# New prices for VectorE's two-operand sums and GpSimd's broadcast products in the table that orders a kernel's queues

## The chip, the cores and the metric

The kernel runs on one core of one Trainium2 chip. The metric is the device time of one execution in microseconds (us). Five queues matter: TensorE (PE in the profile, with its weight loads as PEld), VectorE (DVE), ScalarE (ACT), GpSimd (POOL), and SyncE (SP), which issues the DMA transfers. Each queue runs its instructions in the order in which they stand in it; an instruction whose input isn't ready holds up all behind it.

## What is computed

Eight sequences of 4224 positions with 192 channels. A dynamic convolution with seven taps per position and head (eight heads of 24 channels), the taps normalised by a softmax; then the real part of a two-dimensional Fourier transform added to its own input; then a layer norm and a two-layer perceptron (192 to 768 to 192) with a second residual:

```python
w = np.exp(weight_gen - max)                      # softmax over the 7 taps
w = w / (np.sum(w, axis=-1, keepdims=True) + 1e-09)
x = einsum('bshk,bskhg->bshg', w, x_unfolded)     # dynamic convolution
X = np.fft.fft(x, axis=1)
X = np.fft.fft(X, axis=2)
u = x + np.real(X)
un = (u - mu) / np.sqrt(var + 1e-06)
ch = np.maximum(un @ w_ch1, 0.0) @ w_ch2
return u + ch
```

The inputs are float32; the two weight matrices come as float64 words, which the kernel turns into float32 and then into pairs of float16 (a high and a low part) with a common scale.

## The kernel before

**The stages of a batch.** The 4224 positions of a batch lie as 128 partitions by 33 rows. Batches follow each other as a pipeline: while the perceptron of one batch runs on TensorE, the convolution of the next runs on VectorE and GpSimd.

1. *Taps* (`softmax_taps`, `scale_taps`): VectorE takes maxima, differences, sums and reciprocals of the taps, ScalarE the exponential. For the first two batches this goes by parts (lines 573 to 582), for later ones the maxima and differences (573, 574) are made for the whole batch at once and the sums by quarter (822 to 825). Line 693 scales the taps of the chunks whose products GpSimd makes alone.
2. *Convolution* (`conv` for batches 0 and 1, `wide_conv` from batch 2): a product of the rows with one tap, broadcast over a head's 24 channels, and a sum of the seven. Products are VectorE's (line 762, 768 elements wide; line 847, 1536 wide) or, for a few chunks of batches 0 and 1, GpSimd's (line 760). Sums are GpSimd's (lines 771 and 851); in batch 1, from the third chunk on, the first sum of each chunk is VectorE's (`DVE_ADDS`, also line 771: six of them). In batch 0 TensorE makes some sums.
3. *Fold and spectrum*: GpSimd folds the rows (794, 795), TensorE makes the first transform over positions (pg, line 803), ScalarE and VectorE combine it (809; 810, 813) into gt, which goes to DRAM and comes back in another layout as g (line 889).
4. *Transform*: TensorE's second transform (pp, line 899), copied by ScalarE into pq (903 to 914).
5. *Mix*: TensorE's transform over channels (eo, line 930); ScalarE copies one half (ot, line 935), VectorE adds it to u (936 to 939, 943, 944).
6. *Norm*: ScalarE takes the two statistics of the four rows of a group (lines 965 and 967, one pass per row, into "junk"), a root (969), the normalised rows (996) and their float16 part (1000); GpSimd takes the rest of the parts (1001, 1003); a DMA transposes them into ht.
7. *Perceptron*: nine groups per batch. TensorE makes ph (lines 1060 and 1027), ScalarE evicts it through the ReLU as hh (1075 or 1079; VectorE's line 1080 takes the low part from the eighth group of the program on), TensorE makes po (1094), VectorE adds it to u (1099), and u is stored. PSUM has three banks for ph, two for po, two for transforms and mixes ("fft"), one for the taps of a batch.

The weights of the second layer are turned into float32 (w2f), scaled by their maximum (lines 446 to 461) and split into w2h and w2l (line 489 makes w2l on VectorE, three instructions), while the perceptron of batch 0 runs on w2f.

**What sets the order of the queues.** The program is written stream by stream. At its end `plan` reorders every queue: `cost` gives each instruction two numbers, how long it holds its queue and when its result is there; `walk` then places all instructions one by one by these numbers, the dependencies, the free buffers and banks and a rank. It goes backward and forward over the program ten times, ranks by the lateness that the last pass found, keeps the order with the least total, and ties each queue to that order. So a number in `cost` changes no instruction, only places. For VectorE the number is 150 ns and 1.042 ns for each element of a partition, for GpSimd 183 ns and 2.13 ns (1.92 ns with a float16 output).

Of the kernel before, what the change touches and what calls it, by code (L numbers as in the profile page):

```python
# [11 lines left out]
F16 = mybir.dt.float16  # L12
# [72 lines left out]
def area(ap, kind):  # L85

    if kind == "psum":
        return (0, P), [(0, 1)]
    dims, base, parts, size = [list(d) for d in ap.ap], ap.offset, (0, 1), BYTES[ap.dtype]
    if kind != "dram":  # L90
        step, n = dims.pop(0)
        parts, base = ((base // step, base // step + n), base % step) if step else ((0, P), base)
    free, run = [], 1
    for step, n in dims:
        base += min(step, 0) * (n - 1)
        if n > 1 and step:
            free.append((abs(step), n))
    free.sort(reverse=True)
    while free and (free[-1][0] <= run or np.prod([n for _, n in free]) > 80):
        step, n = free.pop()  # L100
        run += step * (n - 1)
    spans = [base]
    for step, n in free:
        spans = [b + step * k for k in range(n) for b in spans]
    if len(spans) == 2 and run >= 4 * 192:
        spans, run = [min(spans)], run + max(spans) - min(spans)
    return parts, sorted((b * size, (b + run) * size) for b in spans)


def meet(a, b):  # L110

    (pa, sa), (pb, sb) = a, b
    if pa[0] >= pb[1] or pb[0] >= pa[1] or sa[0][0] >= sb[-1][1] or sb[0][0] >= sa[-1][1]:
        return False
    i = j = 0
    while i < len(sa) and j < len(sb):
        if sa[i][0] < sb[j][1] and sb[j][0] < sa[i][1]:
            return True
        if sa[i][1] <= sb[j][1]:
            i += 1  # L120
        else:
            j += 1
    return False


def covers(a, b):

    (pa, sa), (pb, sb) = a, b
    return len(sa) == 1 and pa[0] <= pb[0] and pb[1] <= pa[1] and sa[0][0] <= sb[0][0] and sb[-1][1] <= sa[0][1]


def together(ap):

    run = 1
    for step, n in reversed(ap.ap[1:]):
        if n > 1 and step != run:
            break
        run *= n
    return run


def cost(ins, lane, reads, writes):

    count = lambda ap: int(np.prod([n for _, n in ap.ap[1:]]))
    out = writes[0]
    n = max(map(count, reads + writes))
    if lane == "pe":
        n = count(out)
        t = 2 * max(112 if 64 < n <= DH else 56, 0.855 * n) if reads[0].dtype == F32 else max(55.8, 0.417 * n + 2.4)
        if reads[0].dtype == F16 and reads[0].ap[0][1] == P // 2:  # L150
            t = HALF
        return t, t + 178
    if lane == "sp":
        if ins.opcode == "DmaTransposeAnt":
            return TURN, 2000 + 1.2 * n, 1.09 * n
        size, run = BYTES[out.dtype], min(together(ap) for ap in reads + writes)
        return 400, 2000 + WIRE * count(out) * size, out.ap[0][1] * count(out) / run * (0.5 + 0.0023 * run * size)
    if lane == "dve":
        t = 150 + (6.27 if ins.opcode == "Reciprocal" else 1.042) * n + (60 if len(reads) == 3 and n < 512 else 0)
        return t - 83, t  # L160
    if lane == "pool":
        t = 183 + (1.92 if out.dtype == F16 else 2.13) * n
        return t - 45, t
    t = 190 + (0.833 if out.ap[-1][0] == 1 else 1.666) * n + 90 * (len(reads) - 1)
    return (t + 100, t + 90) if len(writes) > 1 else (t - 95, t)


def plan(nc, tc, homes, holds, glued, opening):

    ops, index = [], {}  # L170
    writers, readers, users = defaultdict(list), defaultdict(list), defaultdict(list)
    rows = defaultdict(list)
    for at, ins in enumerate(nc.cur_bb.bb.instructions):
        reads, writes = ([a.bass_ap for a in args if hasattr(a, "bass_ap")] for args in (ins.ins, ins.outs))
        if ins.engine not in LANES or not writes:
            continue
        joined = ins.name in glued
        k, lane = index.setdefault(ins.name, len(ops) - joined), LANES[ins.engine]
        spots = [(ap.tensor.name, area(ap, homes[ap.tensor.name][0]), w)
                 for w, aps in ((0, reads), (1, writes)) for ap in aps if ap.tensor.name in homes]  # L180
        needs = {}
        for name, spot, w in spots:
            psum = homes[name][0] == "psum"
            for old, sync in ((writers[name], True), (readers[name], w)):
                for other, j in old if sync or psum else ():
                    if j != k and (psum or meet(spot, other)):
                        needs[j] = needs.get(j, False) or sync
        for name, spot, w in spots:
            kind, tag, bufs = homes[name]
            if name not in users and bufs and kind != "dram":  # L190
                rows[kind, tag].append(name)
            users[name].append(k)
            if w and homes[name][0] != "psum":
                for old in (writers, readers):
                    old[name] = [(other, j) for other, j in old[name] if not covers(spot, other)]
            (writers if w else readers)[name].append((spot, k))
        for lo, hi, first in holds:
            if lo <= at < hi and first.engine == ins.engine:
                needs.setdefault(index[first.name], False)
        price = cost(ins, lane, reads, writes)  # L200
        if joined:
            line, _, paid, wants, names = ops[k]
            for j, sync in needs.items():
                wants[j] = wants.get(j, False) or sync
            ops[k] = (line + [ins], lane, (paid[0] + price[0], paid[0] + price[1]), wants, names | {n for n, _, _ in spots})
        else:
            ops.append(([ins], lane, price, needs, {n for n, _, _ in spots}))
# [139 lines left out]
def tile_dynconv_fnet_mlp(  # L347
# [859 lines left out]
    for b in range(B):  # L1207
# [6 lines left out]
        for g in range(NG):  # L1214
            if b > 0 or g >= QUICK:
                at = t0 - mix_at + step * g + (0.7 if b == 0 else 0)
                add(at, at + step, late_mix(g) if b == 0 and g >= QUICK else mix(b, g))
                add(max(at + step, t0 + g - 2.0), t0 + g - 1.0, norm(b, g))
    run()
    plan(nc, tc, homes, holds, glued, last_pq0)  # L1220


# [35 lines left out]
```

## Time and profile before

| | |
|---|---|
| runs | 1088.95, 1089.6, 1089.92 us (median 1089.6) |
| span of the profiled execution | 1087.9 us; 1.7 us of the median lie around it |
| instructions | 23453 |
| TensorE busy | 1065.5 us (98%) |
| VectorE busy | 958.7 us (88%) |
| GpSimd busy | 857.1 us (79%) |
| ScalarE busy | 800.0 us (74%) |
| DMA queue, share of 16 engines | 45.2% |

The profile is that of one execution. Its page has busy times by engine, the span in 40 slices, the chain of waits that ended last, and the costliest groups of instructions. The trace behind it was read by stretches of time, by line, and as a timeline of single instructions. A row of the timeline has the start (us), the length (us), the engine, the line, the operation, and output<-inputs with their shapes; in brackets stands how long the engine stood idle just before, and whose result ended that. Busy times of TensorE are of pipelined matmuls and somewhat generous.

### The profile page before, as it was taken

What the parts mean: (1) busy time and instruction counts of PE and PEld (TensorE: products, weight loads), DVE (VectorE), ACT (ScalarE), POOL (GpSimd) and SP (SyncE); (2) the same over time, 40 slices, a digit from 0 to 9 for tenths busy, and PEclk for the clock granted to TensorE, in tenths of its full rate; (3) what the DMA queues carried; (4) which work ended last, traced back from release to release, by engine and by line L of the source; (5) the groups of instructions that cost most, each with busy time, mean ns of one, the idle gap of its engine ahead of it and who ended that gap; (6) DMA issues with size and microseconds to landing.
All of it is one profiled execution on the core that took longest, in us unless ns stands there. A gap on an engine that the chain in (4) does not pass through costs nothing.

```text
span 1087.9 us, 23453 instructions
## 1 busy us (share of the span) xinstructions
PE 1065.5 (98%) x8600; PEld 802.9 (74%) x8600; DVE 958.7 (88%) x1639; ACT 800.0 (74%) x2414; POOL 857.1 (79%) x615
## 2 busy tenths in 40 slices
PE   7899999999999999999999999999999999999998
PEld 5477777787767877777778876887778777786767
DVE  8999999899989999899999999899999998355543
ACT  4666864679966878788786877678786878588842
POOL 5989699899969999799969999699969999011200
PEclk9999999999999999999999999999999999999999
DMA  9353135714492348623582348624582333623311
GB/s 323 129 146 115 34 94 141 202 46 111 119 259 80 85 115 206 170 67 85 129 248 79 92 109 220 157 57 121 122 205 68 83 68 89 140 56 76 79 53 48
DMA packets 171091, 131.20 MB, mean 121 GB/s; under 512 B 119067, under 2 KB 151776, under 8 KB 170976
## 3 DMA queue, kind: packets, MB, share of 16 engines
q1 hardware_dynamic: 170976, 129.70, 45.2%
q8 instruction: 68, 1.11, 0.4%
q14 instruction: 47, 0.39, 0.1%
HBM read 61.46 MB, written 39.37 MB: 93 GB/s over the span
## 4 chain that ended last, share of the span: by engine, by line
PE 66%; DVE 14%; POOL 5%; DMA 4%; ACT 3%; issue 3%; SPq 0%; DVEq 0%; ACTq 0%; POOLq 0%
PE po L1094 27%; PE ph L1060 24%; PE pp L899 5%; PE eo L930 4%; PE ph L1027 3%; DVE pr L847 3%; POOL u L771 2%; PE pg L803 2%; DVE hh L1080 2%; ACT pr L723 1%; DMA ht<-hl 1%; DVE pr L762 1%; POOL u L851 1%; DMA g<-g_d 1%; DMA ring<-ht 1%
## 5 line engine op out<-in xcount | busy, mean ns | idle before, releaser
L851 POOL TENSOR_TENSOR u<-u,pr 128x1536 f32<-128x1536 f32 x144 | 497.0, 3452 | 5.5 <-DVE pr L847 1.7
L1094 PE MATMUL po<-w2h,hh 128*128 128x192 f16 x2832 | 409.2, 247 | 0.0
L1094 PEld LDWEIGHTS <-hh 128*128 128x128 f16 x4248 | 359.1, 98 | 60.1 <-issue 15.2
L1060 PE MATMUL ph<-ht,w1h 128*128 128x512 f16 (+1 forms) x1296 | 382.7, 362 | 0.3 <-ACT ht L987 0.3
L1094 PE MATMUL po<-w2l,hh 128*128 128x192 f16 x1416 | 348.8, 246 | 0.0
L1080 DVE SCALAR_TENSOR_TENSOR hh<-ph,hh 128x512 f16<-128x512 f32 (+1 forms) x390 | 240.5, 636 | 60.9 <-ACT hh L1079 60.5
L1079 ACT ACTIVATE hh<-ph 128x512 f16<-128x512 f32 (+1 forms) x390 | 206.0, 550 | 89.2 <-PE ph L1060 41.0
L847 DVE TENSOR_TENSOR pr<-x_sb,wp 128x1536 f32<-128x1536 f32 x144 | 249.7, 1747 | 7.3 <-POOL u L851 7.3
L1060 PEld LDWEIGHTS <-w1h 128*128 128x128 f16 x1296 | 125.3, 98 | 97.9 <-issue 9.4
L1060 PE MATMUL ph<-ht,w1l 128*128 128x512 f16 (+1 forms) x528 | 181.7, 350 | 0.0
L996 ACT ACTIVATE un<-u,rs 128x192 f32<-128x192 f32 x252 | 122.2, 539 | 40.2 <-POOL rs L994 34.5
L1001 POOL TENSOR_TENSOR hl<-un,hl 128x512 f16<-128x512 f32 (+1 forms) x69 | 74.9, 1086 | 84.3 <-issue 42.5
L771 POOL TENSOR_TENSOR u<-u,pr 128x768 f32<-128x768 f32 (+1 forms) x72 | 117.9, 1649 | 12.2 <-DVE pr L762 11.4
L967 ACT ACTIVATE junk<-u,st 128x192 f16<-128x192 f32 x252 | 114.3, 453 | 4.4
L965 ACT ACTIVATE junk<-u 128x192 f16<-128x192 f32 x252 | 90.8, 360 | 27.6 <-DVE u L939 21.8
L1099 DVE SCALAR_TENSOR_TENSOR u<-po,isc,u 128x384 f32<-128x384 f32 (+1 forms) x122 | 73.1, 599 | 21.1 <-PE po L1094 20.7
L930 PEld LDWEIGHTS eo<-cs_sb,pq 97*128 97x128 f32 x544 | 78.3, 191 | 13.4 <-issue 4.4
L930 PE MATMUL eo<-cs_sb,pq 97*128 97x97 f32 x544 | 85.7, 275 | 0.0
L762 DVE TENSOR_TENSOR pr<-x_sb,wp 128x768 f32<-128x768 f32 (+1 forms) x91 | 74.7, 868 | 2.1 <-POOL u L771 0.7
L1060 PEld LDWEIGHTS <-w1l 128*128 128x128 f16 x528 | 51.9, 98 | 21.6 <-issue 0.5
L794 POOL TENSOR_TENSOR sm<-u 128x382 f32<-128x382 f32 x64 | 64.6, 1009 | 3.7 <-ACT u L779 3.2
L994 POOL TENSOR_TENSOR rs<-st,rs 128x4 f32<-128x4 f32 (+1 forms) x69 | 13.6, 201 | 67.4 <-DVE rs L970 67.3
(130 smaller groups left out, 1538.4 us busy)
## 6 DMA issues: line engine op xcount, KB each, us to landing
out_dram<-u SPq DMA_DIRECT2D x64, 384.0 KB
x_sb<-in_x_dram SPq DMA_DIRECT2D x48, 384.0 KB
g<-g_d SPq DMA_DIRECT2D x40, 336.0 KB
x_sb<-in_x_dram SPq DMA_DIRECT2D x8, 864.0 KB
g_d<-gt SPq DMA_DIRECT2D x32, 195.0 KB
g_d<-gt SPq DMA_DIRECT2D x32, 189.0 KB
w<-in_weight_gen_dram SPq DMA_DIRECT2D x6, 924.0 KB
x_sb<-in_x_dram SPq DMA_DIRECT2D x8, 672.0 KB
```

The source lines that it names most:

```text
L762: last_product[b] = nc.vector.tensor_tensor(out=dst, in0=rows, in1=wk, op=ALU.mult)
L771: adder.tensor_tensor(out=u, in0=u, in1=pr, op=ALU.add)
L847: last_product[b] = nc.vector.tensor_tensor(out=pr.rearrange("p (s r) (h g) -> p s (r h) g", s=2, g=G), in0=rows, in1=wp[:, :, :, k:k + 1] ...
L851: nc.gpsimd.tensor_tensor(out=u, in0=u, in1=pr, op=ALU.add)
L930: last_mix[b] = nc.tensor.matmul(eo[:, e, j, :], lhsT=pq[0:DH, e, r, r:r + P], rhs=cs_sb[:, e, :], start=True, stop=True)
L965: nc.scalar.activation(junk, uv[t], AF.Identity, scale=-1.0 / D, accum_out=st[:, t, 0:1])
L967: nc.scalar.activation(junk, uv[t], AF.Square, bias=st[:, t, 0:1], accum_out=st[:, t, 1:2])
L996: nc.scalar.activation(un[:, t, :], uv[t], AF.Identity, bias=rs[:, 1, t:t + 1], scale=rs[:, 0, t:t + 1])
L1060: last_ph[n] = nc.tensor.matmul(ph[:, 0:T], lhsT=wt[:, cs_], rhs=ht[:, 0:T, blk], start=(i == 0 and not opens), stop=(i == len(terms) - 1 ...
L1079: nc.scalar.activation(a[:, 0:T], ph[:, 0:T], AF.Relu)
L1080: nc.vector.scalar_tensor_tensor(out=l[:, 0:T], in0=ph[:, 0:T], scalar=0.0, in1=a[:, 0:T], op0=ALU.max, op1=ALU.subtract)
L1094: nc.tensor.matmul(po[t // 2][:, t % 2, :], lhsT=hx[:, t], rhs=wx[:, c2, :], start=(c2 == 0 and i == 0), stop=(c2 == NH - 1 and i == len(t ...
```

## The change

`cost` gets the names of all tiles that don't lie in PSUM. A VectorE instruction that reads exactly two operands of more than 64 elements, both of them outside PSUM and neither broadcast along its last axis, is priced at 2.0 ns per element in place of 1.042. A GpSimd instruction with a broadcast operand is priced at 1.78 ns per element in place of 2.13. All else is as before.

```diff
-def cost(ins, lane, reads, writes):
+def cost(ins, lane, reads, writes, sbuf):
...
     if lane == "dve":
-        t = 150 + (6.27 if ins.opcode == "Reciprocal" else 1.042) * n + (60 if len(reads) == 3 and n < 512 else 0)
+        slow = len(reads) == 2 and n > 64 and all(ap.tensor.name in sbuf and ap.ap[-1][0] for ap in reads)
+        t = 150 + (6.27 if ins.opcode == "Reciprocal" else 2.0 if slow else 1.042) * n + (60 if len(reads) == 3 and n < 512 else 0)
         return t - 83, t
     if lane == "pool":
-        t = 183 + (1.92 if out.dtype == F16 else 2.13) * n
+        t = 183 + (1.92 if out.dtype == F16 else 1.78 if any(ap.ap[-1][0] == 0 for ap in reads) else 2.13) * n
         return t - 45, t
...
-    rows = defaultdict(list)
+    rows, sbuf = defaultdict(list), {name for name, home in homes.items() if home[0] != "psum"}
...
-        price = cost(ins, lane, reads, writes)
+        price = cost(ins, lane, reads, writes, sbuf)
```

The first rule meets the six adds of line 771 in batch 1; the second meets the nineteen products of line 760 in batches 0 and 1, and two small products of tap tables. Line 489 reads three operands (w2f, a scale, w2h) and keeps its price. The two programs hold the same instructions; from the 61st place on TensorE's queue and the 67th on VectorE's the order differs nearly everywhere by a few places, and TensorE's last 915 or so are the same again. The changed kernel's lines are higher by one (the eviction of line 1075 is line 1076). Three places follow. A row has the line, the operation, and output<-inputs with their tiles' names and running numbers.

ScalarE, near the end of the perceptron's second group: hh_1_4 and hh_1_5 are its last two evictions, rs_3 and un_3 the norm of group 3, junk_4 the passes over the rows of group 4, ot_5 a copy of a mix. Before:

```order
L969 ACTIVATE rs_3_1225<-st_3_1224,eps_t 128x4
L996 ACTIVATE un_3_1227<-u_2_228,rs_3_1225 128x192 x4
L1000 CAST hl_3_1273<-un_3_1227 128x4x192
L1075 ACTIVATE hh_1_4_1302<-ph_1_4_1296 128x512
L1075 ACTIVATE hh_1_5_1314<-ph_1_5_1308 128x512
L935 COPY ot_5_1400<-eo_5_1358 128x194
L965 ACTIVATE junk_4_1341,st_4_1339<-u_4_337 128x192 x3
L1075 ACTIVATE hh_2_0_1328<-ph_2_0_1322 128x512
```

And with the change:

```order
L997 ACTIVATE un_3_1227<-u_2_228,rs_3_1225 128x192 x4
L936 COPY ot_5_1400<-eo_5_1358 128x194
L1001 CAST hl_3_1273<-un_3_1227 128x4x192
L966 ACTIVATE junk_4_1341,st_4_1339<-u_4_337 128x192 x4
L968 ACTIVATE junk_4_1341,st_4_1339<-u_4_337,st_4_1339 128x192 x4
L970 ACTIVATE rs_4_1340<-st_4_1339,eps_t 128x4
L1076 ACTIVATE hh_1_4_1302<-ph_1_4_1296 128x512
L1076 ACTIVATE hh_1_5_1314<-ph_1_5_1308 128x512
```

The eight passes of group 4 and their root moved ahead of the two evictions; before they stood between the evictions that follow.

VectorE, where the scale of the second layer's weights is made and the taps of batch 2 begin (w_2042 are these taps; po_3_1 the second half of the output of group 3). Before:

```order
L1099 SCALAR_TENSOR_TENSOR u_2_228<-po_3_1_1730,sc_w_879,u_2_228 128x384
L461 TENSOR_SCALAR sc_w_1803<-m_w_1796 128x1
L459 TENSOR_SCALAR sc_w_1803<-m_w_1796 128x1
L529 TENSOR_TENSOR isc<-sc_w_879,sc_w_1803 128x1
L762 TENSOR_TENSOR pr_8_3_2009<-x_sb,wp_815 128x192 x2
L762 TENSOR_TENSOR pr_8_5_2016<-x_sb,wp_815 128x192 x2
L573 TENSOR_REDUCE wp_2041<-w_2042 128x264
L574 TENSOR_TENSOR w_2042<-w_2042,wp_2041 128x1848
```

And with the change:

```order
L763 TENSOR_TENSOR pr_8_3_2009<-x_sb,wp_815 128x192 x2
L763 TENSOR_TENSOR pr_8_5_2016<-x_sb,wp_815 128x192 x2
L574 TENSOR_REDUCE wp_2041<-w_2042 128x264
L575 TENSOR_TENSOR w_2042<-w_2042,wp_2041 128x1848
L1100 SCALAR_TENSOR_TENSOR u_2_228<-po_3_1_1730,sc_w_879,u_2_228 128x384
```

The add of po_3_1, which gives its bank free, moved behind the last products of batch 1 and the two wide rows of the taps; the scale rows moved further back still.

VectorE, in the first quarter of batch 2's convolution (pr_0_3 to pr_0_6 are products 1536 wide; w2l the low part of the second layer's weights). Before:

```order
L847 TENSOR_TENSOR pr_0_3_2189<-x_sb,wp_2041 128x1536
L1099 SCALAR_TENSOR_TENSOR u_4_337<-po_4_1_1914,sc_w_879,u_4_337 128x384
L847 TENSOR_TENSOR pr_0_4_2235<-x_sb,wp_2041 128x1536
L1099 SCALAR_TENSOR_TENSOR u_4_337<-po_5_0_1975,sc_w_879,u_4_337 128x384
L847 TENSOR_TENSOR pr_0_5_2266<-x_sb,wp_2041 128x1536
```

And with the change:

```order
L848 TENSOR_TENSOR pr_0_3_2189<-x_sb,wp_2041 128x1536
L1100 SCALAR_TENSOR_TENSOR u_4_337<-po_4_1_1914,sc_w_879,u_4_337 128x384
L848 TENSOR_TENSOR pr_0_4_2235<-x_sb,wp_2041 128x1536
L490 SCALAR_TENSOR_TENSOR w2l<-w2f,sc_w_1803,w2h 128x384
L1100 SCALAR_TENSOR_TENSOR u_4_337<-po_5_0_1975,sc_w_879,u_4_337 128x384
L490 SCALAR_TENSOR_TENSOR w2l<-w2f,sc_w_1803,w2h 128x384 x2
L848 TENSOR_TENSOR pr_0_5_2266<-x_sb,wp_2041 128x1536
```

The three w2l rows, which stood as one run nine places ahead of the batch's first product (u_0), moved in between its fifth and sixth.

## Prediction

> **What bounds the kernel now.** I read the head of the page first, then the windows of the span by stage, then the groups of waits.
>
> ```profile
> span 1087.9 us, 23453 instructions
> PE 1065.5 (98%) x8600; PEld 802.9 (74%) x8600; DVE 958.7 (88%) x1639; ACT 800.0 (74%) x2414; POOL 857.1 (79%) x615
> ```
>
> TensorE is busy for 98% of the span and every other engine has air over the whole of it. A new order issues the same matmuls, so it can win only what PE loses in waits, and it loses only where some new wait reaches PE. Where those waits are, the windows say (start and end in us, length, busy time of each engine):
>
> ```profile
> core 0: us, PE busy (x) PEld busy (x) DVE busy (x) ACT busy (x) POOL busy (x), PEclk, DMA share, GB/s
> 0.00:100.00 100.00, 89.12 (x445) 62.35 (x446) 92.95 (x191) 56.86 (x225) 82.91 (x73) 0.98 0.60 194
> 100.00:205.00 105.00, 100.19 (x562) 75.77 (x562) 102.00 (x178) 72.82 (x189) 93.69 (x77) 1.00 0.36 98
> 205.00:935.00 730.00, 727.13 (x6249) 552.32 (x6248) 691.77 (x1130) 572.91 (x1710) 663.76 (x440) 1.00 0.49 125
> ```
>
> PE is idle for 10.9 us in the head (filling, loads), for 105 − 100.19 = 4.8 us in 100 to 205, where the second batch is convolved, and for 730 − 727.13 = 2.9 us in all the steady part. In 100 to 205 VectorE is busy for 102.00 of 105 us: there the two engines bound each other, and there all repriced instructions stand. A better order can thus gain about 4.8 + 2.9 = 7.7 us at the very most outside the head; a worse one has no such bound. The waits of PE by kind (sum, count, longest):
>
> ```profile
> PE po L1094 <- DVE u L1099: 2.2, 2, 1.4
> PE pg L803 <- POOL sm L795: 2.1, 3, 1.3
> PE pp L899 <- DMA g<-g_d: 1.5, 2, 0.9
> PEld pp L899 <- DMA g<-g_d: 1.4, 1, 1.4
> ```
>
> The first two are of the stretch 100 to 205, the last two lie where a batch's transform begins.
>
> **What is repriced.** The rule for VectorE meets six instructions, the adds of line 771 in batch 1: the walk counted 150 + 1.042 × 768 = 950 ns for each, and now 150 + 2.0 × 768 = 1686. The rule for GpSimd meets the products of line 760: 183 + 2.13 × 768 = 1819 ns, now 1550. In the trace (count, shortest/median/longest ns):
>
> ```profile
> L771 DVE TENSOR_TENSOR u<-u,pr x6: 958/1698/2411, 122.0 to 175.6; 128x768 f32<-128x768 f32 x6
> L760 POOL TENSOR_TENSOR pr<-x_sb,w x12: 1542/1580/1593, 72.5 to 108.2; 128x768 f32<-128x768 f32 x12
> L489 DVE SCALAR_TENSOR_TENSOR w2l<-w2f,sc_w,w2h x3: 603/605/953, 194.3 to 195.7; 128x384 f16<-128x384 f32 x3
> L851 POOL TENSOR_TENSOR u<-u,pr x144: 3422/3452/3486, 204.4 to 911.3; 128x1536 f32<-128x1536 f32 x144
> ```
>
> Both new prices are better averages. The product's is a constant of the instruction (1542 to 1593). The add's is not: 958 to 2411 ns for one shape is a wait, and the timeline shows for what:
>
> ```profile
> 142.15 1.83 POOL L771 TENSOR_TENSOR u<-u,pr 128x768 f32<-128x768 f32 x1
> 142.38 2.41 DVE L771 TENSOR_TENSOR u<-u,pr 128x768 f32<-128x768 f32 x1
> 143.92 1.88 POOL L1001 TENSOR_TENSOR hl<-un,hl 128x512 f16<-128x512 f32 x1
> ```
>
> ```profile
> L1001 POOL TENSOR_TENSOR hl<-un,hl 128x512 f16<-128x512 f32 x61 | 71.5, 1172 | 75.8 <-ACT hl L1000 38.3 <-issue 34.1 <-DMA ht<-hl 2.8
> ```
>
> VectorE's add starts at 142.38 inside GpSimd's add, which ends at 143.98; the add ends at 144.79, 0.81 us later, so it did its work after GpSimd's. GpSimd's next instruction takes 1.88 us where its group's mean is 1.172: it stood behind the VectorE add in turn. So an add costs about 0.96 us plus what is left of GpSimd's instruction, and the table now holds the mean of that. The instructions themselves become neither shorter nor longer; only places in the queues change. The rest is what the moves cost.
>
> [...]
>
> **The moves, one by one.**
>
> *VectorE, 70 us: the tap scaling of batch 1.* The two line-693 rows now stand behind about eleven rows of the first weight preparation, some 4.5 us later. GpSimd's first product of batch 1 waits for the first of them, so GpSimd's run of products starts later by that. It is covered: after those products GpSimd has nothing to do until VectorE's products arrive.
>
> ```profile
> 70.50 0.39 DVE L693 TENSOR_TENSOR w<-w,wp 128x224 f32<-128x224 f32 x1
> ...
> 123.94 1.82 POOL L771 TENSOR_TENSOR u<-u,pr 128x768 f32<-128x768 f32 x1 [8.41 <-DVE pr L762]
> ```
>
> The wait of 8.41 us shrinks to about 4. Cost **0**; without that cover 4.5 us.
>
> *ScalarE, 83 us.* The weight conversion of line 488 goes ahead of the copies of the transform's fifth piece, and the chain copies, first mixes, first norm stands behind it.
>
> ```profile
> 83.49 0.58 ACT L488 ACTIVATE w1h<-pw_w,sc_w 128x384 f16<-128x384 f32 x1 [0.50 <-DVE pw_w L483]
> 91.30 0.32 ACT L935 COPY ot<-eo 128x194 f32<-128x194 f32 x1 [0.78 <-PE eo L930]
> 92.02 0.36 DVE L936 TENSOR_TENSOR eo<-eo,ot 128x194 f32<-128x194 f32 x1
> ```
>
> The copies are pushed by 0.58 to 1.08 us (the conversion, with or without its own wait); VectorE takes the first mix 92.02 − 91.62 = 0.40 after it is ready, so 0.2 to 0.7 us comes through. I take **+0.4**.
>
> *ScalarE, 128 to 134 us.* Before, the evictions of ph_1_4 and ph_1_5 start at 128.70 and the eight statistics passes of group 4 are spread between later evictions. Now all eight, and the root behind them, stand ahead of these evictions.
>
> ```profile
> 128.70 1.09 ACT L1075 ACTIVATE hh<-ph 128x512 f32<-128x512 f32 x2
> 130.23 0.36 ACT L965 ACTIVATE junk<-u 128x192 f16<-128x192 f32 x1
> 130.72 0.36 ACT L965 ACTIVATE junk<-u 128x192 f16<-128x192 f32 x1
> 131.45 0.38 PE L1060 MATMUL ph<-ht,w1h 128*128 128x512 f16 x1
> 138.84 0.61 DVE L1099 SCALAR_TENSOR_TENSOR u<-po,sc_w,u 128x384 f32<-128x384 f32 x1
> 139.11 0.46 ACT L967 ACTIVATE junk<-u,st 128x192 f16<-128x192 f32 x1
> 139.59 0.73 PE L1094 MATMUL po<-w2f,hh 128*128 128x192 f32 x3 [1.36 <-DVE u L1099]
> 145.38 0.92 PE L1094 MATMUL po<-w2f,hh 128*128 128x192 f32 x4 [0.80 <-DVE u L1099]
> ```
>
> A first pass takes 0.49 from start to start (130.23, 130.72), a second 0.46 and the same gap of 0.13. Four of each: 1.96 + 2.36 = 4.3 us; with the mix's copy (0.32, row at 91.30) and as much for the root 4.9, so the first eviction ends near 128.70 + 4.9 + 0.55 = 134.2. PE wants that bank at 131.45: a new wait of 2.75 us. In return VectorE's line 1099 moves ahead by several rows, from 138.84 to about 134.6, and both po waits of 1.36 and 0.80 end. Net **+0.6**; bounds +2.75 (they stay) and −2.2 (the eviction is no later).
>
> *But GpSimd sets the pace here.* These +1.0 us stand ahead of a wait that GpSimd decides:
>
> ```profile
> 175.13 0.92 PE L803 MATMUL pg<-sm,f_sb 128*128 128x192 f32 x4 [1.33 <-POOL sm L795]
> ```
>
> Of the 105 us from 100 to 205 GpSimd is idle for 11.3, and 8.4 of these are the gap before 123.94: from there on it hardly stops, and its own order is the same but for a few places. PE arriving 1.0 us later waits 0.33 us instead of 1.33. So of the two terms **0** is left; if GpSimd's sum comes later too, +1.0.
>
> *VectorE, 187 to 194 us: one bank given back late.* Line 1099 of po_3_1 now stands behind the two rows that begin the tap softmax of batch 2.
>
> ```profile
> 187.22 0.60 DVE L1099 SCALAR_TENSOR_TENSOR u<-po,sc_w,u 128x384 f32<-128x384 f32 x1
> 189.49 2.09 DVE L573 TENSOR_REDUCE wp<-w 128x264 f32<-128x1848 f32 x1
> 191.61 2.08 DVE L574 TENSOR_TENSOR w<-w,wp 128x1848 f32<-128x1848 f32 x1
> 192.41 0.33 PE L1094 MATMUL po<-w2f,hh 128*128 128x192 f32 x1
> ```
>
> Those two end at 193.69 now; without line 1099 and the four small scale rows ahead of them (1.1 us) at about 192.6. Line 1099 then ends at 193.2, and PE's po_4_1, which takes this bank, is due at 192.41. Wait: **+0.9** with the hop (bounds 0, if PE is late itself, and +2.2, if the 1.1 us is not won).
>
> *VectorE, 207 to 217 us: the w2l splits.* Three line-489 rows, which ran among short GpSimd rows at 194.3 to 195.7, now stand between the products of batch 2's first quarter, beside GpSimd's adds of 3.45 us.
>
> ```profile
> 207.91 1.75 DVE L847 TENSOR_TENSOR pr<-x_sb,wp 128x1536 f32<-128x1536 f32 x1 [0.90 <-POOL u L851]
> 211.71 1.75 DVE L847 TENSOR_TENSOR pr<-x_sb,wp 128x1536 f32<-128x1536 f32 x1 [1.51 <-POOL u L851]
> 215.37 1.75 DVE L847 TENSOR_TENSOR pr<-x_sb,wp 128x1536 f32<-128x1536 f32 x1 [1.91 <-POOL u L851]
> ```
>
> VectorE waits here for GpSimd, 0.90 + 1.51 + 1.91 = 4.3 us in three gaps, and the splits' 1.8 us of work fit in. If each of the first two waits for half an add (1.7 us), the sum is 5.2, which VectorE regains by the 1.8 us it no longer spends at 194. Cost **0**; bounds 0 and +4.4 (rival below).
>
> *The starts of the transforms.* In most batches from the second on the line-899 matmuls stand one to two matmul groups earlier in PE's queue, and the spectrum's last tile also somewhat earlier in VectorE's. PE's two kinds of waits for g, 1.5 + 1.4 = 2.9 us in three places, may end or double. **0**, bounds −2.9 and +2.9.
>
> **Sum.** 0 + 0 (0.4 + 0.6, swallowed) + 0.9 + 0 + 0 = +0.9 us on the profiled span of 1087.9, so 1088.8. The median of the runs is 1089.6, 1.7 us above that span (what lies around it is untouched), so the forecast is **1090.5 us**. A difference under 0.2% (2.2 us, so 1087.4 to 1091.8) can't be told from no change in a measurement of this kernel.
>
> **Rivals.**
>
> *The reckoning pays: faster.* With better means the walk puts line 1099 and the folds where they are needed: the waits of 1.36, 0.80 and 1.33 us vanish without a new one, 3.5 us: 1086.1. For it: two of the three should end by my own walk through the queues. Against: the 1.33 is GpSimd's, whose work did not shrink, and at 128 and 192 us I see banks given back later.
>
> *The splits stand behind GpSimd's adds: slower.* At 207 us the first line-489 row waits out one add (3.45), the second, behind a line-1099 row, the next one (3.45); the third runs free, since GpSimd then waits for the product queued behind it. With 1.8 us of work that is 8.7 us in a stretch with gaps of 4.3: VectorE 4.4 us late, and the evictions of group 7 and GpSimd's adds behind it. It decides as soon as more than 1.3 us of it reaches PE; in full 1090.5 + 4.4 = 1094.9. For it: the add at 142.38. Against: the first splits had 603 and 605 ns next to a GpSimd busy 94 of 105 us, and PE has a group of matmuls in hand there.
>
> *The transforms run ahead of their data: slower.* If the three waits for g become six at the same 1 us each, +2.9: 1093.4. For it: these matmuls move earlier in several batches. Against: a PE that is late by 0.9 has less to wait for.
>
> *Nothing that PE notices:* the walk's order moves only rows with slack: 1089.6.
>
> **Chances.** The forecast 0.42; nothing noticed 0.06; the splits 0.16; the transforms 0.15; faster 0.21. The forecast's own spread (−1.5 to +2) puts a little over either bound: faster 0.23, same 0.43, slower 0.34. With cases on both sides the likeliest one's own range is 1089 to 1092.5; the range that holds 8 in 10 goes from the faster rival, 1086.1, to a little past the splits', 1095.5.
>
> **What would show it.** Right: in the changed profile GpSimd's wait near 124 us is 3 to 5 us; an eviction of line 1076 ends near 134 with PE waiting for ACT about 2.7 us near 131; the two po waits near 139 and 145 are gone; one po wait near 193 is about 1 us; the pg wait near 175 is under 0.5. Wrong: PE's busy time in the stretch 205 to 935 falls by more than 2 us against its length (then the splits, visible as line-490 rows of 2 us or more, or g waits, visible in their group), or the stretch 100 to 205 loses under 3 us (then the reckoning pays). The six adds will again spread from about 0.96 to over 2 us; if they all took 1.7, the price per element would be right after all.

## The result: slower, and the profile after

The changed kernel takes 1097.5 us (median of five runs, 1096.1 to 1100.0) against 1089.6 before (1088.4 to 1090.4): a ratio of 1.008, 95% interval 1.0065 to 1.0094. Forecast were 1090.5 us, a range of 1086.1 to 1095.5, and no change as the likeliest. The profiled execution has a span of 1098.2 us; it is the longest of the five. A second measurement of the same kernel (changed_again below) gave a ratio of 1.0075 (1.0053 to 1.0098) and a span of 1094.4. Five executions of 1111 to 2196 us, three of them of the kernel before, are in no ratio.

The windows of the changed kernel, read as those of before (start and end, length, busy time of each engine, the TensorE clock that was granted):

```profile
0.00:100.00 100.00, 90.48 (x446) 63.91 (x447) 92.59 (x192) 57.48 (x226) 78.09 (x70) 0.98 0.60 194
100.00:205.00 105.00, 98.73 (x535) 75.14 (x535) 94.00 (x170) 71.39 (x187) 95.27 (x78) 0.95 0.34 98
205.00:935.00 730.00, 722.98 (x6179) 548.24 (x6179) 695.12 (x1127) 567.18 (x1700) 664.99 (x438) 1.00 0.49 122
```

Two things differ in 100 to 205 us. TensorE issues 535 matmuls instead of 562, though its busy time is only 1.5 us shorter; and the clock column, 1.00 before, says 0.95. The waits of PE over 1 us in that stretch are two, and neither was among those before (sum, count, longest):

```profile
PE po L1095 <- DVE m_w L451: 3.5, 1, 3.5
PE po L1095 <- DVE gt L814: 2.6, 1, 2.6
PE ph L1061 <- ACT ht L988: 0.3, 1, 0.3
```

In the timeline both are waits for a PSUM bank that VectorE gives back late:

```profile
121.61 0.30 ACT L810 COPY up<-pg 128x190 f32<-128x190 f32 x1
...
128.84 0.35 DVE L811 TENSOR_TENSOR gt<-pg,up 128x194 f32<-128x194 f32 x1
129.41 0.35 DVE L814 TENSOR_TENSOR gt<-pg,up 128x190 f32<-128x190 f32 x1
129.81 5.85 PE L1095 MATMUL po<-w2f,hh 128*128 128x192 f32 x24 [2.58 <-DVE gt L814]
...
186.05 0.60 DVE L1100 SCALAR_TENSOR_TENSOR u<-po,sc_w,u 128x384 f32<-128x384 f32 x1
186.71 0.50 PEld L1095 LDWEIGHTS po<-w2f,hh 128*128 128x128 f32 x2 [3.96 <-DVE u L1100]
186.71 1.00 PE L1095 MATMUL po<-w2f,hh 128*128 128x192 f32 x2 [3.47 <-DVE m_w L451]
```

At 127 us po_0_1 needs the bank of pg_0, the first spectrum tile of batch 1, which alone lies in a po bank. ScalarE had copied its half at 121.9, but VectorE took the rest only at 128.84 to 129.76, behind nine products and mixes. At 183 us po_4_0 needs the bank of po_3_0, whose add on VectorE comes at 186.05; before, it came at 182.35 and TensorE did not wait:

```profile
182.35 0.61 DVE L1099 SCALAR_TENSOR_TENSOR u<-po,sc_w,u 128x384 f32<-128x384 f32 x1
183.86 1.46 PE L1094 MATMUL po<-w2f,hh 128*128 128x192 f32 x8
```

(Of the changed kernel's two rows, the matmul's names a row on VectorE that ended just after that add; the weight load's names the add itself.)

The clock by fine windows (length, PE busy, granted clock, share of DMA, GB/s):

```profile
126.00:130.00 4.00, 1.42 (x11) 1.00 0.01 2
130.00:131.00 1.00, 1.00 (x6) 0.82 0.37 95
131.00:132.00 1.00, 1.00 (x5) 0.50 0.67 169
134.00:135.00 1.00, 1.00 (x7) 0.98 1.10 135
183.00:185.00 2.00, 0.24 (x2) 1.00 0.50 120
185.00:186.00 1.00, 0.00 (x0) 0.62 1.02 393
187.00:192.00 5.00, 5.00 (x15) 0.50 0.94 317
192.00:193.00 1.00, 1.00 (x6) 0.96 0.93 308
```

With each of the two waits the granted clock falls to 0.50: behind the first from about 130.6 to 134.0 (3.4 us, which costs 1.7 us of work), and from about 185.2, inside the second, to 192.1 (6.8 us, 3.4 us of work). The 24 matmuls of po_0_1 take 5.85 us there; 24 of the same form took 4.14 us before. A third place is later: the w2l splits.

```profile
L490 DVE SCALAR_TENSOR_TENSOR w2l<-w2f,sc_w,w2h x3: 654/2752/3652, 211.7 to 218.5; 128x384 f16<-128x384 f32 x3
...
210.59 3.47 POOL L852 TENSOR_TENSOR u<-u,pr 128x1536 f32<-128x1536 f32 x1
211.72 2.75 DVE L490 SCALAR_TENSOR_TENSOR w2l<-w2f,sc_w,w2h 128x384 f16<-128x384 f32 x1
214.72 3.44 POOL L852 TENSOR_TENSOR u<-u,pr 128x1536 f32<-128x1536 f32 x1
214.92 4.23 DVE L490 SCALAR_TENSOR_TENSOR w2l<-w2f,sc_w,w2h 128x384 f16<-128x384 f32 x2
...
246.32 0.88 PE L931 MATMUL eo<-cs_sb,pq 97*128 97x97 f32 x6 [1.41 <-DVE gt L814]
```

The first split starts inside GpSimd's add and ends at 214.47, 0.41 us after it (214.06); the second does the same at 218.57 against 218.16; the third starts at 218.50, when GpSimd has only 0.24 us of a short row left, and takes 0.65. Before, three took 0.60, 0.61 and 0.95. At the end of this quarter's products VectorE is 5.3 us late against before (next row at 222.51, before 217.16), 2.2 of which it brought along (first product at 201.65, before 199.41), and TensorE waits 1.4 us for a mix's bank at 245.

**The ledger.** For each run stands below what TensorE lost from 100 to 250 us in its profile: idle time (length less busy), and slow clock (length times one less the clock), both from windows of 20 to 50 us. Before: 5.0 idle (0.31 + 1.36 + 2.00 + 1.15 + 0.14), no slow clock. Changed: 7.7 idle (0.23 + 2.58 + 0 + 3.47 + 1.41) and 5.3 slow (1.80 + 3.50). The difference is 2.7 + 5.3 = 8.0 us, and the medians differ by 7.9. (The windows give the clock with two digits; by its edges the slow clock is 1.7 + 3.4 = 5.1.) In this profile two thirds of the loss is not waiting but the clock behind it. Over many executions it is nearer to half: in the second measurement the timed runs have a mean clock of 0.9938, those of before 0.9974, and 0.0036 of the span are 3.9 of the 8.2 us between the means. That waits and slow clock are the whole account, the profiles show: the span less all idle time of TensorE and less its slow clock is 1063.2 us before, 1063.7 and 1063.0 in the two profiles of the changed kernel, and 1061.7 to 1064.9 in twelve others (1066.4 in filled_wait, with its 3.0 of filling).

| run | what it is | ratio to before (95%) | idle, slow clock, us | more than before, us |
|---|---|---|---|---|
| changed_again | the changed kernel | 1.0075 (1.0053 to 1.0098) | 7.8, 5.3 | 8.1 |
| dve_price | VectorE's price alone | 1.0032 (1.0019 to 1.0044) | 5.3, 5.0 | 5.3 |
| pool_price | GpSimd's price alone | 1.0018 (1.0006 to 1.0031) | 6.0, 0 | 1.0 |
| early_add | changed, po_3_0 earlier | 1.0045 (1.0029 to 1.0060) | 8.0, 0 | 3.1 |
| filled_wait | changed, wait at 183 filled | 1.0046 (1.0028 to 1.0064) | 4.4, 1.8, and 3.0 of filling | 4.3 |
| bank_early | changed, pg_0 earlier | 1.0053 (1.0035 to 1.0071) | 7.8, 5.3 | 8.1 |
| bank_and_eviction | and two evictions earlier | 1.0048 (1.0032 to 1.0065) | 8.0, 3.5 | 6.5 |
| splits_early | changed, w2l earlier | 1.0043 (1.0025 to 1.0060) | 6.0, 5.3 | 6.4 |
| all_three | the last two and early_add | 1.0025 (1.0009 to 1.0041) | 5.8, 1.6 | 2.4 |
| all_four | and po_0_0 earlier | 1.0035 (1.0020 to 1.0050) | 5.6, 1.75 | 2.4 |
| late_3 | before, one add later | 1.0031 (1.0015 to 1.0046) | 6.9, 0 | 1.9 |
| late_4 | before, that add later still | 1.0072 (1.0049 to 1.0096) | 10.0, 3.5 | 8.5 |
| old_then_new | old order to 314 us, then new | 1.0013 (0.9999 to 1.0027) | 5.0, 0 | 0.1 |
| new_then_old | the reverse | 1.0078 (1.0047 to 1.0108) | 9.2, 3.5 | 7.7 |

The ledger is of one execution and the ratio of all: 0.001 of ratio is 1.1 us, and a ratio is known to 1.4 to 3.3 us, so that two neighbours in the table often overlap.

### The profile page after: what moved, and what is told of

The parts are those of the page before. It is cut to its first block, busy times and chain, and to the rows that moved or that the text cites. A ratio compares the mean times of both kernels' runs of the same rounds, so it can differ in the third digit from the quotient of the medians.

```text
span 1098.2 us, 23479 instructions
## 1 busy us (share of the span) xinstructions
PE 1072.2 (98%) x8600; PEld 807.6 (74%) x8600; DVE 959.4 (87%) x1639; ACT 801.4 (73%) x2414; POOL 857.6 (78%) x615
## 4 chain that ended last, share of the span: by engine, by line
PE 74%; DVE 11%; POOL 5%; DMA 4%; issue 4%; ACT 2%; SPq 0%; POOLq 0%; DVEq 0%; ACTq 0%
PE po L1095 30%; PE ph L1061 26%; PE eo L931 5%; PE pp L900 5%; PE ph L1028 4%; POOL u L772 3%; DVE pr L763 3%; PE pg L804 3%; DMA g<-g_d 2%; DVE pr L848 1%; PE pa L768 1%; DMA g_d<-gt 1%; DVE hh L1081 1%; PE tr L987 1%; DMA ht<-hl 1%
## 5 line engine op out<-in xcount | busy, mean ns | idle before, releaser
L1095 PE MATMUL po<-w2f,hh 128*128 128x192 f32 x336 | 64.9, 339 | 6.0 <-DVE m_w L451 3.5
```

Source lines behind the costliest of these rows:

```text
L1095: nc.tensor.matmul(po[t // 2][:, t % 2, :], lhsT=hx[:, t], rhs=wx[:, c2, :], start=(c2 == 0 and i == 0), stop=(c2 == NH - 1 and i == len(t ...
```

## The experiments

The edits that move rows stand behind the walk; `move(queue, rows, before)` takes the named rows out of a queue and puts them ahead of another row, `at(queue, out, in)` finds rows by their tiles (with the batch's number first). All other rows stay. The lines of these kernels are higher by 14 or more than those of the changed one.

**Which price.** Each of the two alone:

```diff
-        t = 183 + (1.92 if out.dtype == F16 else 1.78 if any(ap.ap[-1][0] == 0 for ap in reads) else 2.13) * n
+        t = 183 + (1.92 if out.dtype == F16 else 2.13) * n
```

> Only the VectorE price is changed (2.0 ns per element for sums of two operands outside PSUM); GpSimd's price is that of the kernel before. Theory A (the time is lost where this one order lets TensorE wait over 2.5 us, at 127 and at 183 us, each wait followed by some us at half the granted clock): this order is another one, so its time is what its own waits make it; if the VectorE price alone brings the two late rows on VectorE, 1094 to 1099, else near 1090. Theory B (the new VectorE price is at fault, since an add is no longer placed where GpSimd is idle): the same loss as the whole change, about 1097.

```diff
-        t = 150 + (6.27 if ins.opcode == "Reciprocal" else 2.0 if slow else 1.042) * n + (60 if len(reads) == 3 and n < 512 else 0)
+        t = 150 + (6.27 if ins.opcode == "Reciprocal" else 1.042) * n + (60 if len(reads) == 3 and n < 512 else 0)
```

> Only GpSimd's price of broadcast products is changed (1.78 ns per element); VectorE's price is that of the kernel before. Theory A: near 1090 if its order has no wait of TensorE over 2.5 us, and 3 to 7 us more for each one it has. Theory B (the VectorE price is at fault): 1089 to 1091.

Measured 1.0032 and 1.0018. The order with VectorE's price has a wait of 2.3 us for a transposed ht at 179 us, another of 0.8 soon after, and the slow clock behind them (0.80 in 175 to 200 us, 5.0 us lost); that with GpSimd's has no wait over 1.8 us and no slow clock (1.00 from 100 to 250 us). Neither is the changed order, so their losses are not parts of its loss. Theory B, that the loss is VectorE's price, does not hold: that price alone gives less than half of it (1.0032, with the whole change 1.0075).

**The wait at 183 us, taken away and filled.**

```diff
+    move("dve", at("dve", "mx_w2")[1:] + at("dve", "ex_w2") + at("dve", "u_0_2", "po_0_3_0") + at("dve", "m1_w2"), at("dve", "pr_1_7_5")[0])
```

> The changed kernel, with five VectorE rows (the add of po_3_0, which frees a bank of po, and the four rows of the weight maximum ahead of TensorE's mr_w) moved ahead of the last products of batch 1; nothing else. Theory A: TensorE's wait of 3.5 us at 183 us ends, the granted clock stays 1.00 from 180 to 195 us, TensorE loses 5 to 6 us less by 200 us; up to half of it may come back at 212 to 245 us, where VectorE is late by the w2l splits: 1091 to 1095. Theory C (the loss is that of the w2l splits and of the transforms behind them): within 1 us of 1097.5, since VectorE is then what everything waits for.

```diff
+                for _ in range(14 if (n, c) == (5, 0) else 0):
+                    idle.append(nc.tensor.matmul(ph[:, 0:T], lhsT=w1h0[:, cs_], rhs=ht[:, 0:T, 0], start=True, stop=True).ins)
...
+    first = at("pe", "ph_0_5_0")[0]
+    order["pe"][first:first] = idle
```

> The changed kernel, with the wait at 183 us filled: 14 repeats of the first matmul of ph_5_0 (their result is overwritten) ahead of that group, some 3.5 us of TensorE work, so that TensorE reaches po_4_0 when its bank comes free. The waiting itself stays as long. Theory A: no drop of the granted clock at 185 to 193 us, and the time falls by what that drop cost, about 3.4 us: 1094. If the clock costs nothing: 1097.5 or a little more.

The two come out alike, 1.0045 and 1.0046. (The fourteen matmuls took 3.0 us, not 3.5, so 0.4 us of the wait is left.) Windows of early_add, then of filled_wait:

```profile
130.00:140.00 10.00, 9.19 (x53) 1.00 0.48 98
185.00:190.00 5.00, 3.80 (x22) 1.00 0.87 250
190.00:195.00 5.00, 3.95 (x22) 1.00 0.94 345
```

```profile
130.00:140.00 10.00, 10.00 (x51) 0.87 0.48 98
185.00:190.00 5.00, 4.57 (x23) 1.00 0.94 298
190.00:195.00 5.00, 5.00 (x30) 1.00 0.68 252
```

filled_wait removes nothing: TensorE comes to po_4_0 as late as before and has done 3.0 us of useless work. Still the ratio is 0.0029 below the changed kernel's 1.0075, some 3 us, as expected from the clock alone. The two intervals overlap (with the first measurement's, 1.0065 to 1.0094, they don't); that the clock is a cost of its own rests on the full clock in these windows and on late_3 below as well. The mean clocks of the timed runs agree: 0.9962 in filled_wait and 0.9968 in early_add against 0.9938 in the changed kernel, which is 2.6 and 3.3 us of clock. In early_add the wait is gone and the clock full; new waits of 1.0 to 1.4 us at 152, 186 and 193 us take part of the gain. Its window 130 to 140 has a surprise: the wait at 128 us is 2.57 us long there too, and no slow clock follows (1.00 in this window); the last section comes back to it.

**The wait at 127 us: layers.**

```diff
+    move("dve", at("dve", "gt_1_0", "pg_1_0"), at("dve", "pr_1_2_1")[1])
```

> The changed kernel, with the two VectorE rows that take pg_0 of batch 1 out of its bank moved ahead by eleven rows, to about 122.5 us; nothing else. Theory A: po_0_1 no longer waits at 127 us, but the wait does not end: TensorE comes to ph_2_1 at about 131.5 and waits there for ScalarE's eviction of ph_1_4, which stands behind the eight statistics passes, until about 134.5: 3.0 us, and the clock drops again. So the time stays within 2 us of the changed kernel's, ratio 1.006 to 1.010. If the bank was the whole cause: 3 to 4 us less, ratio 1.004 to 1.005.

```diff
+    move("act", at("act", "hh_0_1_4") + at("act", "hh_0_1_5"), at("act", "junk_0_4")[0])
```

> The same, and ScalarE's two evictions of ph_1_4 and ph_1_5 ahead of the eight passes of group 4. Theory A: neither wait over 1 us is left from 125 to 140 us, the clock stays 1.00 there, and TensorE loses 3 to 4.5 us less by 140 us. Part of it comes back, since GpSimd sets the pace up to 175 us and the changed kernel lost nothing there from 140 to 175 (the kernel before 2.4): ratio 1.005 to 1.008.

PE's waits from 100 to 205 us in bank_early, then in bank_and_eviction:

```profile
PE po L1109 <- DVE m_w L465: 3.5, 1, 3.5
PE ph L1075 <- ACT hh L1090: 2.7, 1, 2.7
```

```profile
PE po L1110 <- DVE u L1115: 3.6, 1, 3.6
PE po L1110 <- DVE m_w L466: 3.0, 1, 3.0
```

In bank_early the 2.6 us for the bank became 2.7 us for ScalarE's eviction, with the same slow clock (0.91 in 120 to 140 us in both), and the ledger is unchanged. With the evictions moved as well, TensorE waits 3.6 us at 132 us for the add of po_0_0. My expectation that no wait over 1 us would be left was wrong: I had not looked behind the second wait. The ratios of both are lower than the changed kernel's by some 2.5 us, which is at the edge of what the intervals tell; both lie below the ranges expected by theory A.

**The splits.**

```diff
+    move("act", at("act", "w2h"), at("act", "un_0_7")[0])
+    move("dve", at("dve", "w2l"), at("dve", "pr_2_0_1")[0])
```

> The changed kernel, with the three w2l rows of VectorE moved ahead of batch 2's second product (to about 203.5 us, where GpSimd has nothing to run), and ScalarE's three w2h rows ahead of the norm of group 7; nothing else. [...] If a two-operand row of VectorE is slow by itself and not by GpSimd: they take the same 7 us and nothing changes.

```profile
L505 DVE SCALAR_TENSOR_TENSOR w2l<-w2f,sc_w,w2h x3: 607/609/612, 203.5 to 204.5; 128x384 f16<-128x384 f32 x3
```

The same three instructions take 0.61 us each from 203.5 us on, where they took 2.75, 3.65 and 0.65 beside GpSimd's adds, and the wait at 245 us is gone. VectorE is 2.5 us earlier behind the quarter's products (219.97 against 222.51). The ratio is 1.0043, about 3.5 us less than the changed kernel's (the intervals overlap); the ledger accounts for 1.4 to 1.8 of it. The rest I can't place.

**All together.**

> The changed kernel with all these moves together: the bank of pg_0 and the two evictions near 125 us, the five VectorE rows near 182 us, the w2l splits near 204 us. If these places are the whole of the loss: the time of the kernel before, ratio 0.998 to 1.002. If the transforms that start ahead of their data, or many small shifts, carry a part: 1.002 to 1.006 with no wait over 2 us left.

```diff
+    move("dve", at("dve", "u_0_0", "po_0_0_0"), at("dve", "pr_1_2_5")[0])
```

> As all_three, and VectorE's add of po_0_0 moved ahead by twelve rows, to about 128 us: in all_three TensorE, freed of the first two waits, came to po_1_0 at 132.6 us and waited 3.6 us for this bank. Theory A: that wait and the clock's drop behind it end (5.4 us lost there); GpSimd's pace gives back 2 to 3 us from 140 to 175 us: ratio 0.998 to 1.001. If GpSimd's pace alone sets 175 us: as all_three, 1.0025.

all_three, 1.0025, takes back two thirds of the loss; its longest wait is the 3.6 us at 132 us. all_four ends that one and gains nothing: TensorE now waits 1.6 us at 139 us for ScalarE and 3.0 us at 149 us for the next add, with the slow clock behind it (0.95 in 140 to 175 us). That is not the 0.998 to 1.001 that was expected, so what is left in all_three, some 2.7 us, stays open.

**The reverse: the loss made in the kernel before.** One row of the old order moved, and the same with four small products ahead of it:

```diff
+    move("dve", at("dve", "u_0_2", "po_0_3_0"), at("dve", "u_0_8", "eo_0_8")[2])
```

> The kernel before, with one row of VectorE moved: the add of po_3_0 stands eighteen rows later, at about 186 us instead of 182.35. TensorE then waits at 184 us for 2.5 to 3 us. Theory A: 2.5 us of waiting, less 0.9 of a later wait that it swallows, and in some executions 1.7 us of slow clock: ratio 1.001 to 1.003.

```diff
+    move("dve", at("dve", "pr_1_8_3") + at("dve", "pr_1_8_5") + at("dve", "u_0_2", "po_0_3_0"), at("dve", "u_0_8", "eo_0_8")[2])
```

> The same with four small products ahead of that add as well: TensorE waits 3.5 to 5 us. Theory A: a wait over 3.4 us always brings the slow clock, so the loss is more than the wait: 4 us of waiting and 1.7 to 3.4 us of slow clock, less about 1 us swallowed later: ratio 1.004 to 1.006. If the clock does not follow the length of the wait: 1.002 to 1.004.

Windows of late_3, then of late_4:

```profile
185.00:190.00 5.00, 2.16 (x12) 1.00 0.91 253
190.00:195.00 5.00, 5.00 (x29) 1.00 0.95 343
```

```profile
185.00:190.00 5.00, 0.00 (x0) 0.98 0.93 248
190.00:195.00 5.00, 4.14 (x12) 0.50 0.65 238
195.00:200.00 5.00, 5.00 (x24) 0.83 0.63 217
```

The late add alone (eleven rows later in the trace, at 187.19) makes a wait of 3.0 us and costs 0.31% (0.15 to 0.46); with the four products the wait is 6.0 us, longer than expected, and the whole costs 0.72%, nearly the loss of the whole change, from five rows of one queue. In the profile of late_3 the clock stays at 1.00, but not in every execution: of its twelve timed runs the nine with a mean clock of 0.996 to 0.998 took 1089.6 to 1091.9 us, the three with 0.994 took 1092.9 to 1095.3. The same program is thus some 3 us longer where the clock was slow for longer; 0.003 of the span are 3.3 us. For late_4, six of six have 0.994 or 0.995.

**Where in the program.** At about 314 us both orders have placed the same instructions on every queue, so they can be joined there:

```diff
+    cut = dict(pe=1351, dve=533, act=569, pool=214, sp=147)
+    order = {lane: old[lane][:cut[lane]] + new[lane][cut[lane]:] for lane in cut}
```

> The kernel's order before the change up to about 314 us (where both orders have placed the same instructions on each of the five queues), the changed order behind it. If the loss lies at the waits of batch 1 alone (theory A): ratio 0.999 to 1.001. If the changed order of the later batches costs by itself, as the rest in all_three suggests: 1.002 to 1.004.

The reverse has `new` and `old` exchanged:

> The reverse: the changed order up to about 314 us, the order from before behind it. Theory A: nearly the whole loss, ratio 1.006 to 1.008, with the waits at 127, 183 and 245 us as in the changed kernel. If the later batches carry a part: 1.003 to 1.006.

The old order up to 314 us with the new one behind it is not distinguishable from before (1.0013, 0.9999 to 1.0027); the new one up to there carries the whole loss (1.0078). So it lies in the first 314 us. That the later batches cost up to 0.27% by themselves is not excluded, and would explain what is left in all_three. (In the profile of new_then_old the wait at 128 us, 2.57 us, has no slow clock behind it (1.00 from 120 to 175 us), as in early_add.)

> The changed kernel itself, beside the others on one chip. Ratio 1.006 to 1.010. In its profile the two waits at 127 and 183 us are there with the same lengths (2.6 and 3.5 us) and the clock drops after the second; the wait of 2.4 us for g at 698 us, if it belongs to the order, is there again, and if it is of that one execution, is not.

The same waits of 2.6 and 3.5 us came again with the same slow clock (0.91 in 120 to 140 us, 0.86 in 175 to 200). The matmuls' wait for g at 698 us, 2.3 us, did not (0.8 us): that one, with a slow clock of its own behind it (0.66 in 700 to 705 us), belonged to the one execution of 1098.2 us.

## Why the prediction was wrong, point by point

- *A bound.* "A new order can win only what PE loses in waits, and it loses only where some new wait reaches PE": right as to the place. It left out that a wait can cost more than its length. The sum had a term for each wait and none for the clock, and 5.3 of the 8.0 us are that. (Of the waits for sm in its list only the one of 1.3 us lies in 100 to 205; the other two, 0.8 us together, come ahead of it.)
- *VectorE at 70 us, cost 0:* right. GpSimd's wait near 124 us is 3.09 us (4 were forecast) and still covers.
- *ScalarE at 83 us, +0.4:* nothing of it is seen; TensorE begins the first mixes at 89.85 us, before at 89.95.
- *ScalarE at 128 us, +0.6:* the mechanism was right and hidden. bank_early shows the wait, 2.7 us where 2.75 was forecast. That ph_1_4 is evicted near 134 in the changed profile too is chance: ScalarE is through with the passes and the root at 132.8, as in bank_early, where the eviction starts at 132.9; here it then waits 1.15 us for TensorE. And pg_0's bank, which I had not followed, was late first: a wait of 2.58 us that has no term in the sum. Of the two po waits that end, 1.36 and 0.80 us, the changed profile shows neither.
- *GpSimd sets the pace, so these terms are swallowed:* right. From 140 to 175 us TensorE idles 0.0 us after and 2.0 before, so most of the 2.58 + 1.80 us lost at 127 us against 1.36 before come back (2.8 us more than before are lost by 140 us, 0.9 by 175).
- *One bank given back late at 192 us, +0.9:* the wrong add. The sum followed po_3_1, which is late too, but TensorE never comes to it on time: po_3_0's add, which stands only four rows further back in VectorE's queue than before, came 3.7 us later, and TensorE stood there for 3.5 us. This is the step that failed, by 2.6 us of waiting and 3.4 of slow clock. (Its upper bound is 2.0 by its own rows, not 2.2: 193.69 and 0.6 against 192.41, with the same 0.1 for the hop, an estimate; at 139.45 us before, 0.14 us lie between the end of the add and the matmul that waited for it.)
- *The w2l splits, cost 0:* wrong; the half an add in the sum and the whole one in the rival were the author's estimates (before, the one of the three rows that started inside a GpSimd add, a short one of 0.95 us, took 0.95 and ended 0.42 us behind it). The rival was right row by row: the first ends 0.41 us behind an add, the second behind the next, the third runs free (2.75, 3.65 and 0.65 us; 7.0 in all, 8.7 in the rival's sum with the waits taken whole). Its price is not settled: 1.4 us of waiting reached TensorE in the profile, not 4.4, but without it (splits_early) the ratio falls by some 3.5 us. The sign that was named for this rival came: 205 to 935 loses 7.0 us where it lost 2.9, though 2.3 of them are the wait for g of that one execution.
- *The transforms:* no cost in the median that the runs can tell (old_then_new, 1.0013); the waits for g differ from one execution to the next (2.3 and 0.8 us at 698 us in two profiles of the changed kernel).
- *The six adds:* they spread from 0.95 to 1.53 us (mean 1.18, before 1.68), not to over 2. They became shorter without being changed, because they now wait for less of GpSimd's work: at most 0.71 us of it, before up to 1.59. So the new price, 1.69, fits the order from which it was read and not the order that it makes.

## What to carry to other kernels

When a change moves places in queues, list for each PSUM bank who gives it back and where that row stands now, and follow every one of them: near 130 us three banks were late, and each hid the next. Price a wait of TensorE by its length and by the slow clock that may follow: in the profile before and that of the changed kernel no wait up to 1.65 us had any behind it from 20 us to the last matmuls, the one of 2.58 us at 127 us had 1.7 us of it, and the one of 3.5 us at 183 us 3.4. Where such a wait can't be removed, useless matmuls in it may be cheaper than idleness (3.0 us of them in filled_wait: 1.0046, against 1.0075). A mean duration that is made of waits for another engine is no price of an instruction: it changes with the order that it is used to find (the six adds: 1.68 us before, 1.18 after).

## What the hardware showed that I had not expected

TensorE's clock was halved with some waits and not with others of the same length. One of 1.8 us has no slow clock behind it (pool_price, 1.00 up to 250 us); those of 2.26 us (changed kernel at 698 us, 0.66 in 700 to 705 us), 2.3 us (dve_price, 0.80 in 175 to 200) and 2.7 us (bank_early, 0.91 in 120 to 140) have it. Of six at 2.57 or 2.58 us near 127 us four have it (0.91 in 120 to 140 us: the changed kernel, changed_again, filled_wait, splits_early) and two have none (1.00: early_add, new_then_old). Of three at 3.0 us two have it (0.93 in 175 to 200 us in bank_and_eviction, 0.95 in 140 to 175 in all_four), the one in late_3 has none (1.00 in 175 to 200). Seven of 3.5 to 6.0 us all have it: 0.92 and 0.93 in 120 to 140 us for the 3.6 us at 132 us (all_three, bank_and_eviction), 0.86 in 175 to 200 us for the 3.5 us at 183 us (the changed kernel, changed_again, bank_early, splits_early) and for the 6.0 us of late_4.

Equal lengths with and without a slow clock suggest that it matters where a wait falls, and two traces show where. In the profile before, the records of the clock start at 4.70, 11.53, 14.94 and 1086.73 us; in that of the changed kernel at 7.76, 11.17, 14.58, 130.63, 134.05, 185.25, 192.07, 700.66, 704.07 and 1100.02 us. In each of the two all lie within 10 ns of a whole number of steps of 3.4133 us from the first. By these steps, from 20 us to the last matmuls, three in the changed kernel have more than 1.65 us without a matmul: that from 127.22 us has 2.58, that from 181.83 us 2.01, that from 697.25 us 2.26. At the ends of these three, and nowhere else there, the clock falls. Before, no step of that stretch has more than 1.65, and the clock stays at 1.00. (The ends of matmuls are modelled.) The wait of 2.58 us at 127 us lies whole in one step:

```profile
127.22:130.63 3.41, 0.83 (x6) 1.00 0.02 6
130.63:134.05 3.42, 3.42 (x13) 0.50 0.60 167
```

In early_add the windows of that length that begin at 125.80 us have 0.97 and 1.60 us of the 2.57, and the clock stays at 1.00:

```profile
125.80:129.21 3.41, 2.44 (x17) 1.00 0.01 2
129.21:132.63 3.42, 1.82 (x11) 1.00 0.24 56
132.63:136.04 3.41, 3.41 (x21) 1.00 0.68 156
```

That the idle part of a step decides is the author's reading of these figures; what in the chip does it, and at what length between 1.65 and 2.01 us, is not shown. If it holds, a wait of 2.6 us costs its length alone or 1.7 us on top by chance, since the steps began at another place in each of the two traces; one of 3.5 us, longer than a step, has at least 1.75 us in one step wherever it falls.

VectorE's line 490 took 2.75 and 3.65 us when it started inside GpSimd's adds of 3.47 and 3.44 us, and ended 0.41 us behind each of them; in splits_early, from 203.5 us on, the same rows took 0.61 each.
